# First scores from rows summed in place, and the softmax shift as a bias in every exponential

## The chip, the cores and the metric

The kernel runs on one NeuronCore of a Trainium2 chip. The core has five engines that run beside each other and meet through semaphores: TensorE (matmul; "PE" in a profile, its weight loads "PEld"), VectorE ("DVE"), ScalarE ("ACT"), GpSimd ("POOL") and SyncE ("SP"). Transfers are issued from the queues of SP, ACT and POOL. The metric is the device time of one execution in microseconds: 1229.62 us, the median of three runs (1228.37 to 1229.89).

## The reference

Two independent parts are computed, and their results are put side by side in the last axis. Everything is float32.

```python
# part A: a state-space convolution, L = 2048, D = 576, N = 128
dt = exp(log_dt)[:, None]; logdA = dt * (A_re + 1j*A_im); dB = dt * (B_re + 1j*B_im)
K = einsum("dn,dnl,dn->dl", C, exp(logdA[:, :, None] * l), dB).real
y = irfft(rfft(pad(u)) * rfft(pad(K)))[:L] + u * Dskip
# part B: attention with 32 query heads of 18 columns and one shared head of keys and values, S = 2048
q = (x @ wq).reshape(B, S, 32, 18); k = x @ wk; v = x @ wv
p = softmax(einsum(q, k) * 18 ** -0.5)
out = (p @ v).reshape(B, S, 576) @ wo
```

## The kernel before

**Attention.** The 2048 queries are worked in four chunks `c` of 512, the heads in 16 pairs, the keys in 16 blocks `kb` of 128. One step of the inner loop is a head pair and a key block: two score matmuls write a PSUM tile `s` of 128 keys by 2 x 512 queries (`scores`, L446), one ScalarE instruction takes exp of all 1024 columns into `P` (`exponentials`, L455 and L457), and four matmuls by 256 columns, twice, multiply `P` by the values into `ops` (`product`, L755). There are 1024 such steps. Three score tiles exist (`NS = 3`), so steps are issued in rounds of three: the scores of a round, then products of earlier rounds and filler work, then the next round. A score matmul has to wait until the exponential that read its tile three steps ago has ended. Eight `P` tiles exist (`NP`).

Scores are computed with operands split in a rounded part and a rest: the rows of `kaug` hold kh, kl, kh (18 rows each, keys) and the rows of `aug` hold qh, qh, ql (queries), twice, at partitions 0 and 64, one for each head of a pair. Row 54 of `kaug` is one and row 54 of `aug` is minus an upper bound of the scores, so that the shift of the softmax comes out of the matmul itself: 55 rows. Only the first two head pairs of the first chunk take the shift as `bias=self.nb` (L455). The bound comes from the largest key and query magnitudes (`kmax`, `ab`), through a small matmul `up`, its maximum `un`, and a running maximum `u` over all units so far.

**Convolution.** It is cut into 12 blocks of 48 channels. `front` makes the kernel K from factors (`factors`: an exponential of dt, products by VectorE, two sines and an exponential on ScalarE), tables (`tables`) and matmuls (`kgen`); `back` transforms u and K with matmuls by `dft`, multiplies on VectorE, and transforms back.

**What sets the order.** The order on TensorE, ScalarE and VectorE is the one in which the program issues (`manual_schedule`). In the loop, `main` keeps a model clock (`Clock`) with a price for every operation (an exponential costs 0.925 in it), and a planner fills the time that this clock leaves on TensorE with query projections, output projections and convolution work, in pieces (`Stream`). The constants at the top (`RATE`, `CAP`, `LEAST` and others) steer it. Set-up is written out by hand: `Attention.setup` issues the transfers, keeps TensorE busy with three `cold` matmul sets, projects keys (`kps`), values (`vps`) and the first 126 query columns (`qps`) over five pieces `k` of the model axis, then places keys and queries into `kaug` and `aug` by transfers (L306, L393). `conv.begin` interleaves the first ten pieces of the first convolution block. `values` transposes the values, and then `main` begins.

A `matmul4` is one product of 128 columns as four matmuls of 32 columns, which run side by side; `project` does the same with the four chunks of x.

Of the kernel before, what the change touches and what calls it, by code (L numbers as in the profile page):

```python
# [32 lines left out]
NS = 3  # L33
NP = 8


RATE = 1.7223
PACE = 2.6661
AHEAD = 0.6441
TOTAL = 238.4006  # L40
LAST = 660.2161
DEFER = 0.3799
NAUG = 5
LEFT = 1.0372
CAP = 0.5454
DEBT = 0.8847
GROUP = 0.2874
HOLD = 0.3303
LEAD = 0.8335
MOST = 0.7745  # L50
LEAST = 0.5036
NEAR = 0.4134
SLOPE = 0.2673
SOON = 0.5397
URGENT = 7.3595
GAP = 0.2175
GAP_NEW = 0.6686
# [50 lines left out]
class Vector:  # L108
# [21 lines left out]
    def reciprocal(self, out, src):  # L130
        self.k.dve(out, 6.5e-3)
        return self.v.reciprocal(out, src)

# [55 lines left out]
class Attention:  # L189
# [36 lines left out]
    def setup(self, tp, conv):  # L226

# [3 lines left out]
        self.sel = cp.tile([P, 8], F32, name="sel_sb")  # L235
        spread = tp.tile([P, 130], F32, name="spread_sb")
# [3 lines left out]
        self.kmax = cp.tile([P, 1], F32, name="kmax")  # L240
        wkv = tp.tile([P, 6, 64], F32, name="wkv_sb")
        xr = tp.tile([P, 4, 3, CT], F32, name="xr")
# [8 lines left out]
        self.nb = cp.tile([P, 1], F32, name="nb")  # L251
        self.x0 = x0 = self.xp.tile([P, 5, CT], F32, name="x0", tag="x")

        V.memset(cold, 0.0)
        conv.early()
        nc.sync.dma_start(wkv, a["wkv"])
        for k in range(4):
            nc.sync.dma_start(x0[:, k, :], a["xT"][0, :, k, :])
            nc.sync.dma_start(xr[:, k], a["xT"][1:4, :, k, :].rearrange("c p n -> p c n"))
            if k == 0:  # L260
                nc.scalar.dma_start(self.wq[0], a["wq"][0, :, :, :MT[0][1]])
        nc.sync.dma_start(x0[:, 4, :], a["xe"][0])
        nc.sync.dma_start(xe, a["xe"][1])
        nc.scalar.dma_start(self.sel, a["sel"][:, 0:8])
        nc.scalar.dma_start(spread, a["sel"][:, 8:138])
        for t in self.ring[:2]:
            for b in (32, 96):
                nc.gpsimd.memset(t[b:b + 32, :].bitcast(F32), 0.0)
        for b in (54, 118):
            nc.gpsimd.dma_start(self.kaug[b:b + 1, :], a["ones"])  # L270
# [3 lines left out]
        self.ubound, self.first = None, True  # L274
        self.aug = {n: self.ring[n % NAUG] for n in range(64)}
        self.ready, self.od, self.qd = set(), {}, {}
# [4 lines left out]
        conv.begin()  # L281
        fps = self.bank(CT, "cold")
        for _ in range(3):
            matmul4(nc, fps, cold[:, 0:P], cold)
        kps, self.qps = (self.ps_s.tile([P, 2, CT], F32, tag="s", name=n)[:, 0, :] for n in ("kps", "q0_0"))
        self.pv = pv = self.ps_o.tile([P, CT], F32, tag="o", name="vps")

        def project(ps, j, k):
            for c in range(NCH):
                w = wkv[:, 4 + c // 2 if k == 4 else k, j:j + 32]  # L290
                x = (xe if c % 2 else x0[:, 4, :]) if k == 4 else xr[:, k, c - 1, :] if c else x0[:, k, :]
                nc.tensor.matmul(ps[32 * c:32 * c + 32, :], w, x, start=(k == 0), stop=(k == 4), tile_position=(0, 32 * c))
        for k in range(5):
            project(kps, 0, k)
            matmul4(nc, self.qps, self.wq[0][:, k, :], x0[:, k, :], start=(k == 0), stop=(k == 4))
            if k < 2:
                project(pv, 32, k)
        nc.scalar.activation(kh, kps, AF.Copy)
        V.tensor_reduce(km[:, 4:5], kps, axis=AX.X, op=ALU.max, apply_absolute_value=True)
        V.tensor_scalar(km[:, 0:4], spread[:, 126:130], km[:, 4:5], None, op0=ALU.mult)  # L300
        V.tensor_tensor(kl, kps, kh.bitcast(F32), op=ALU.subtract)

        def place(c):
            for r, t in ((0, kh), (36, kh), (18, kl)):
                for b in (0, 64):
                    nc.sync.dma_start(self.kaug[b + r:b + r + 18, c * CT:(c + 1) * CT].bitcast(F32), t[32 * c:32 * c + 18, :].bitcast(F32))  # L306
        place(0)
        pk = self.bank(4, "kmx")
        nc.tensor.matmul(pk[:126, :], spread[:, 0:126], km[:, 0:4], start=True, stop=True)
        for k in range(2, 4):  # L310
            project(pv, 32, k)
        self.side_work = side = Stream(self.side(), self.k, 99.0)
        while self.first:
            side.advance()
        V.tensor_reduce(self.kmax[:126, :], pk[:126, :], axis=AX.X, op=ALU.max)
        while 1 not in self.ready:
            side.advance()
        for c in range(1, NCH):
            place(c)
        side.advance()  # L320

# [3 lines left out]
        project(pv, 32, 4)  # L325
        V.tensor_copy(self.vt, pv)
# [44 lines left out]
    def first_queries(self, ps):  # L371
        nc, V, mn = self.nc, self.V, MT[0][1]
        qh, ql, ab = self.keys[:, 3, :], self.keys[:, 4, :], self.p2.tile([P, 3], F32, tag="ab", name="ab0_0")
        nc.scalar.activation(qh[:mn, :], ps[:mn, :], AF.Copy)
        V.tensor_tensor(ql[:mn, :], ps[:mn, :], qh[:mn, :].bitcast(F32), op=ALU.subtract)
        V.tensor_reduce(ab[:mn, 0:1], ps[:mn, :], axis=AX.X, op=ALU.max, apply_absolute_value=True)
        yield from self.queries(0, 0, qh, ql, ab[:, 0:1])

    def queries(self, c, m, qh, ql, ab):
# [4 lines left out]
        if m == 0:  # L384
            self.qd[c] = self.dr.tile([H, 55, CT], F32, tag="qd", name=f"qd{c}")
        qd = self.qd[c]

        n0 = 4 if (c, m) == (0, 0) else 0
        for row, src in ((0, qh), (18, qh), (36, ql)) if n0 else ():
            for h in range(n0):  # L390
                b = 64 * (h % 2) + row
                q = nc.gpsimd if h // 2 == 1 else nc.scalar if row < 36 else nc.sync
                q.dma_start(self.aug[h // 2][b:b + 18, :].bitcast(F32), src[h * DH:h * DH + DH, :].bitcast(F32))  # L393
# [5 lines left out]
        self.first = False  # L399
        yield "v", 0.0, False  # L400
        aw = self.p2.tile([P, P], F32, tag="aw", name=f"aw{c}_{m}", bufs=1)
        V.tensor_scalar(aw[:mn, :], ab[:mn, 0:1].broadcast_to([mn, P]), self.kmax[:mn, 0:1], None, op0=ALU.mult)
# [3 lines left out]
        matmul4(nc, up, aw[:mn, :], self.sel[:mn, 0:8])  # L406
# [5 lines left out]
        if self.ubound is not None:  # L412
            u2 = self.p2.tile([P, 1], F32, tag="u2", name=f"u2_{c}_{m}", bufs=4)
            V.tensor_tensor(u2, un, self.ubound, op=ALU.max)
            un = u2
        self.ubound = un
        if n0:
            V.tensor_scalar(self.nb, un, -SCALE, None, op0=ALU.mult)
        sh = self.p2.tile([8, CT], F32R, tag="sh", name=f"sh{c}_{m}", bufs=1)
        V.tensor_scalar(sh, un[0:8, 0:1].broadcast_to([8, CT]), -1.0, None, op0=ALU.mult)  # L420
        self.ready.update(range(n0 // 2))
        q = nc.gpsimd if n0 == 0 else nc.sync
        if n0:
            yield "w", 0.0, False
            store(q)
        q.dma_start(qd[h0 + n0:h1, 54, :], sh[:h1 - h0 - n0, :].bitcast(F32))
        self.queried = c * H + h1

    def fetch(self, group):

        while self.next < min(64, 2 * group + NAUG) and 2 * self.next + 2 <= self.queried:
            c, pr = divmod(self.next, 16)
            t = self.aug[self.next]
            for j in range(2):
                self.nc.sync.dma_start(t[64 * j:64 * j + 55, :].bitcast(F32), self.qd[c][2 * pr + j])
# [3 lines left out]
    def scores(self, i, c, pr, kb, cost):  # L439
# [4 lines left out]
        for j in range(2):  # L444
            r = slice(64 * j, 64 * j + 55)
# [4 lines left out]
    def exponentials(self, i, c, pr, kb, ps, ready, free):  # L450
# [3 lines left out]
        if 16 * c + pr < 2:  # L454
            nc.scalar.activation(pt, ps, AF.Exp, scale=SCALE, bias=self.nb)  # L455
        else:
            nc.scalar.activation(pt, ps, AF.Exp, scale=SCALE)  # L457
# [158 lines left out]
    def side(self):  # L616
# [3 lines left out]
        yield from self.first_queries(self.qps)  # L620
# [67 lines left out]
    def main(self, conv, flag):  # L688
# [3 lines left out]
        self.load_wo()  # L692
        K.t = K.v = K.a = self.o_free = 0.0
# [76 lines left out]
        for r in range(0, len(pairs), NS):  # L770
            new = range(r, min(r + NS, len(pairs)))
            self.step = new[-1] // 2
            ss = {}
            for i in new:
# [4 lines left out]
                ss[i] = self.scores(i, c, 2 * g + j, kb, 0.335 if i == r else 0.215)  # L779
# [43 lines left out]
        nc.vector.tensor_scalar(flag, self.ubound[0:1, :], LIMIT / (2 * SCALE), None, op0=ALU.is_le)  # L823
# [86 lines left out]
class Conv:  # L910
# [21 lines left out]
    def setup(self):  # L932
# [3 lines left out]
        self.pos = cp.tile([P, 2, NF], F32, name="pos_sb")  # L936
# [7 lines left out]
    def load(self, k, q=None):  # L944
# [5 lines left out]
        raw = self.p0.tile([P, 6, ND], F32, tag="raw", name=f"raw{k}")  # L950
        dt = self.p0.tile([P, ND], F32, tag="dt", name=f"dt{k}")
        q.dma_start(dt, self.a["ldt"][k * ND:(k + 1) * ND].partition_broadcast(P))
        q.dma_start(raw, self.a["prm"][k])
        self.raw[k] = raw, dt

    def load_u(self, k):
# [3 lines left out]
        ut = self.p0.tile([P, 4, NE], F32, tag="u", name=f"u{k}")  # L960
        if k < 2:
            nc.vector.memset(ut[0:1, 0, 0:1], 0.0)
        dsk = self.p0.tile([P, NE], F32, tag="dsk", name=f"dsk{k}")
        nc.sync.dma_start(ut, self.a["u"][k])
        nc.sync.dma_start(dsk, self.a["dsk"][k].partition_broadcast(P))
        self.ut[k] = ut, dsk
        self.ut_ready[k % 2] = self.k.t + 10.0

    def factors(self, k):
# [4 lines left out]
        raw, dt = self.raw.pop(k)  # L974
# [38 lines left out]
        if k == 0:  # L1013
            nc.scalar.activation(m, m, AF.Exp)
# [130 lines left out]
    def back(self, k, kt):  # L1145
        nc, V, p1, K = self.nc, self.V, self.p1, self.k
        tt = V.tensor_tensor
        ut, dsk = self.ut.pop(k)
# [73 lines left out]
    def early(self):  # L1222
        nc = self.nc
        nc.scalar.dma_start(self.pos, self.a["pos"])
# [4 lines left out]
    def begin(self):  # L1229

        for _ in range(10):
            self.streams[0].advance()
# [141 lines left out]
```

## Time and profile before

| | |
|---|---|
| median of three runs | 1229.62 us |
| profiled execution | 1230.26 us, of which span 1228.0 us |
| mean granted TensorE clock | 0.982 |
| TensorE busy | 1154.1 us (94%) |
| ScalarE busy | 1053.9 us (86%) |
| VectorE busy | 994.9 us (81%) |
| first exponential of the loop starts | 32.81 us |
| last one ends | 1200.88 us |

A row of a group view reads: line, engine, operation, output tile <- input tiles, shapes, count | busy us, mean ns of one | idle time of the engine before them and what ended it. A row of the order of time begins with start and duration in us. An engine name with a q is its queue, which issues transfers. The span is cut into slices or stretches where work by stage is wanted; the granted clock is 1.00 at full speed. Busy time of TensorE overlaps between neighbours, so it is an upper estimate of its work.

### The profile page before, as it was taken

The numbers are of one execution on the slowest core, as the hardware profiler recorded it, in microseconds if no ns is written. First come the engines' busy times: TensorE is split into PE (matmuls) and PEld (weight loads), VectorE is DVE, ScalarE is ACT, GpSimd is POOL, SyncE is SP. The second block draws the span as 40 slices with busy tenths as digits, with TensorE's granted clock in tenths as the row PEclk, the third lists the DMA queues.
The fourth block names the chain that finished last, engine by engine and source line by source line (L and its number), as shares of the span: only waits on it lengthen the run. The fifth ranks groups of instructions, "written<-read, shape, count | busy, mean of one in ns | idle before, by whom it ended". The sixth has DMA issues, their size and how long they took to land.

```text
span 1228.0 us, 40862 instructions
## 1 busy us (share of the span) xinstructions
PE 1154.1 (94%) x17882; PEld 609.0 (50%) x17882; DVE 994.9 (81%) x1674; ACT 1053.9 (86%) x1101; POOL 53.7 (4%) x93
## 2 busy tenths in 40 slices
PE   7999899899899899999899999999989899999997
PEld 1455455455445455455454545555545445455544
DVE  4757996996997897896798698898799799698493
ACT  2789899989888989989887989999988989999991
POOL 2000100100100000000010000000010000000000
PEclk8899999999999999999999989999999999999999
DMA  7532312123242112113033300212222211112201
GB/s 231 160 105 65 108 53 84 36 63 91 67 125 78 51 48 82 36 50 108 25 93 105 95 15 34 83 35 77 78 68 87 78 41 53 63 34 77 63 28 55
DMA packets 55082, 89.84 MB, mean 73 GB/s; under 512 B 14172, under 2 KB 24796, under 8 KB 54387
## 3 DMA queue, kind: packets, MB, share of 16 engines
q1 hardware_dynamic: 43911, 72.46, 18.2%
q0 software_dynamic: 10016, 13.98, 4.4%
q8 instruction: 142, 2.33, 0.8%
q10 hardware_dynamic: 972, 0.74, 0.2%
q14 instruction: 41, 0.34, 0.1%
HBM read 49.28 MB, written 36.50 MB: 70 GB/s over the span
## 4 chain that ended last, share of the span: by engine, by line
PE 66%; DVE 23%; DMA 4%; issue 3%; ACT 3%; SPq 0%; DVEq 0%; ACTq 0%
PE ops L755 25%; PE s L446 18%; PE op L186 5%; PE q L186 4%; DVE ks L116 3%; PE iy L186 3%; PE kg L1082 3%; DVE tab L116 3%; DVE acc L116 2%; ACT P L457 2%; DVE f L116 1%; PE lk L186 1%; PE hu L186 1%; PE hk L186 1%; PE fin L186 1%
## 5 line engine op out<-in xcount | busy, mean ns | idle before, releaser
L457 ACT ACTIVATE P<-s 128x1024 f32<-128x1024 f32 x992 | 942.4, 1028 | 118.1 <-PE s L446 111.4
L755 PE MATMUL ops<-P,v_sb 128*32 128x256 f32 x8192 | 533.2, 382 | 7.9 <-DVE o L120 7.7
L446 PE MATMUL s<-aug,kaug 55*128 55x512 f32 x2048 | 350.9, 439 | 10.8 <-ACT P L457 5.7
L755 PEld LDWEIGHTS ops<-P,v_sb 128*32 128x32 f32 x8192 | 255.9, 110 | 181.0 <-issue 35.0
L446 PEld LDWEIGHTS s<-aug,kaug 55*128 55x128 f32 x2048 | 168.0, 185 | 205.3 <-ACT P L457 100.7
L186 PE MATMUL q<-x,wq_sb 128*32 128x256 f32 (+2 forms) x1480 | 116.2, 413 | 21.8 <-DVE ql L116 14.6
L186 PEld LDWEIGHTS q<-x,wq_sb 128*32 128x32 f32 (+2 forms) x1480 | 48.8, 113 | 71.0 <-issue 40.0
L186 PE MATMUL op<-wo_sb,oT 126*32 126x288 f32 (+1 forms) x1024 | 76.7, 415 | 5.1 <-DVE scu L116 2.5
L116 DVE TENSOR_TENSOR tab<-tab,tt 128x576 f32<-128x576 f32 (+1 forms) x72 | 59.2, 822 | 1.9
L120 DVE COPY ksb<-kg 128x192 f32<-128x192 f32 x48 | 17.5, 364 | 53.1 <-PE kg L1082 52.9
L116 DVE TENSOR_TENSOR tab<-tab 128x576 f32<-128x576 f32 (+1 forms) x72 | 59.0, 819 | 1.2
L116 DVE TENSOR_TENSOR tt<-f,sum 128x576 f32<-128x576 f32 (+1 forms) x72 | 58.7, 816 | 0.0
L116 DVE TENSOR_TENSOR tab<-sum,r 128x576 f32<-128x576 f32 (+1 forms) x72 | 58.7, 815 | 0.0
L116 DVE TENSOR_TENSOR tab<-r,dif 128x576 f32<-128x576 f32 (+1 forms) x72 | 58.7, 815 | 0.0
L396 POOL DMA_DIRECT2D qd<-qh x38 | 24.0, 636 | 733.4 <-DVE qh L120 733.4
L116 DVE TENSOR_TENSOR acc<-acc,pt 128x1728 f32<-128x1728 f32 (+2 forms) x36 | 48.6, 1349 | 0.3
L116 DVE TENSOR_TENSOR pt<-us,ks 128x1728 f32<-128x1728 f32 (+2 forms) x36 | 48.6, 1350 | 0.2
L186 PEld LDWEIGHTS op<-wo_sb,oT 126*32 126x32 f32 (+1 forms) x1024 | 28.9, 110 | 38.7 <-issue 16.9
L116 DVE TENSOR_TENSOR sck<-lk,sck 128x384 f32<-128x384 f32 x48 | 24.5, 551 | 27.8 <-PE lk L186 27.8
L455 ACT ACTIVATE P<-s,nb 128x1024 f32<-128x1024 f32 x32 | 33.1, 1116 | 13.5 <-PE s L446 13.4
L1082 PEld LDWEIGHTS kg<-tab 128*32 128x32 f32 x2304 | 35.8, 110 | 16.5 <-issue 7.4
L1082 PE MATMUL kg<-tab 128*32 128x64 f32 x2304 | 42.1, 220 | 2.0 <-DVE tab L116 0.8
(132 smaller groups left out, 1004.9 us busy)
## 6 DMA issues: line engine op xcount, KB each, us to landing
aug<-qd SPq DMA_DIRECT2D x124, 110.0 KB
od<-o SPq DMA_DIRECT2D x31, 256.0 KB
qd<-qh POOLq DMA_DIRECT2D x30, 252.0 KB, 5.7
u<-u SPq DMA_DIRECT2D x12, 384.0 KB
kd<-ksb SPq DMA_DIRECT2D x12, 384.0 KB
kt<-kd SPq DMA_DIRECT2D x48, 96.0 KB
outa<-u SPq DMA_DIRECT2D x12, 384.0 KB
oT<-od SPq DMA_DIRECT2D x16, 252.0 KB
```

What stands on the lines that cost most here:

```text
L116: return self.v.tensor_tensor(out, *a, **k)
L120: return self.v.tensor_copy(out, *a, **k)
L186: nc.tensor.matmul(ps[j:e], w[:, j:e], x, start=start, stop=stop, tile_position=(0, j))
L396: q.dma_start(qd[h0 + n0:h1, row:row + 18, :], src[n0 * DH:mn, :].bitcast(F32))
L446: nc.tensor.matmul(ps[:, j, :], self.kaug[r, kb * P:(kb + 1) * P], t[r, :], start=True, stop=True)
L455: nc.scalar.activation(pt, ps, AF.Exp, scale=SCALE, bias=self.nb)
L457: nc.scalar.activation(pt, ps, AF.Exp, scale=SCALE)
L755: nc.tensor.matmul(o_ps[32 * j:32 * j + 32, cs], self.v[:, kb, :], pts[2 * n + j // 2][:, j % 2, cs], start=(kb + f == 0), stop=(kb + f == ...
L1082: nc.tensor.matmul(ps[32 * g:32 * g + 32, d, :], t[:, :32], t[:, 32:], start=(j == 0), stop=(j == 1), tile_position=(0, 32 * g))
```

## The change

- **Direct rows.** In set-up, three weight tiles `direct` of 128 columns are made: `direct[0]` holds wk three times for each half (with minus wk in the second place), `direct[1]` and `direct[2]` hold wq of heads 0, 1 and 2, 3 in the same way (minus in the third place). GpSimd zeroes them, VectorE copies the columns. Three more `matmul4` for each k sum x times these into `first` tiles, which have the layout of `kaug` and `aug` already. ScalarE copies each sum in rounded form, and one VectorE instruction with a column of 0 and -1 turns the marked rows into the rest. The transfers that placed chunk 0 of the keys and the first four heads go; those for key chunks 1 to 3 stay, half on SP and half on POOL.
- **Order in set-up.** wkv first, then all of chunk 0 of x, then the other chunks (`xr`). TensorE does four cold sets instead of three, then for each k three direct sums and `qps`, and after that keys and values. The scores of the first two steps (`early`) are issued behind the keys. On VectorE the copies for `direct[1]` and `direct[2]` stand behind `conv.begin(7)`.
- **Shift as bias.** Row 54 goes from `kaug`, `aug` and the stored queries (54 rows). Every exponential takes `bias=self.nb[:, m]`, a column for each unit of 126 query columns, made by one instruction with a running minimum; `sh` and `u2` go, and the tile `aw` shrinks from 128 to 8 columns.
- **Fewer early transfers.** `sel` joins `pos` in one tensor, `ldt` joins `prm`, `dsk` joins `u`, `ones` goes, and `wo` is loaded at the loop's step 60 instead of at its start.
- **Constants of the planner.** Twenty of them get other values, and its clocks start at 2.5 and 0.4 for VectorE and ScalarE.

```diff
-RATE = 1.7223
-PACE = 2.6661
+COLD = 4
+RATE = 1.9482
+PACE = 2.0109
...
-LEFT = 1.0372
-CAP = 0.5454
+LEFT = 1.2228
+CAP = 0.9396
...
-        V.memset(cold, 0.0)
+        nc.sync.dma_start(wkv, a["wkv"])
         conv.early()
-        nc.sync.dma_start(wkv, a["wkv"])
         for k in range(4):
             nc.sync.dma_start(x0[:, k, :], a["xT"][0, :, k, :])
-            nc.sync.dma_start(xr[:, k], a["xT"][1:4, :, k, :].rearrange("c p n -> p c n"))
...
+        def rows(t, src, minus):
+            t = t.rearrange("p k (j c) -> p k j c", j=2)
+            for r in range(3):
+                if r == minus:
+                    V.tensor_scalar(t[:, :, :, 18 * r:18 * r + 18], src, -1.0, None, op0=ALU.mult)
+                else:
+                    V.tensor_copy(t[:, :, :, 18 * r:18 * r + 18], src)
+        rows(direct[0], wkv[:, 0:5, 0:DH].unsqueeze(2).broadcast_to([P, 5, 2, DH]), 1)
+        conv.begin(7)
+        for j in range(2):
+            rows(direct[1 + j], self.wq[0][:, :, 36 * j:36 * j + 36].rearrange("p k (j d) -> p k j d", j=2), 2)
+        conv.begin(3)
...
         for k in range(5):
+            for ps, w in zip(sums, direct):
+                matmul4(nc, ps, w[:, k, :], x0[:, k, :], start=(k == 0), stop=(k == 4))
+            matmul4(nc, qps, self.wq[0][:, k, :], x0[:, k, :], start=(k == 0), stop=(k == 4))
+        for j, (ps, t) in enumerate(zip(sums, (self.kaug[:, 0:CT], self.ring[0], self.ring[1]))):
+            nc.scalar.activation(t, ps, AF.Copy)
+            V.scalar_tensor_tensor(t, ps, spread[:, 130 + (j > 0):131 + (j > 0)], t.bitcast(F32), op0=ALU.mult, op1=ALU.add)
+        V.tensor_reduce(ab[:mn, 0:1], qps[:mn, :], axis=AX.X, op=ALU.max, apply_absolute_value=True)
+        conv.begin(1)
+        for k in order[:3]:
             project(kps, 0, k)
+            project(pv, 32, k)
+        project(kps, 0, 4)
+        project(kps, 0, 3)
+        self.early = {i: self.scores(i, 0, i, 0, 0.0) for i in range(2)}
...
+        for c in range(1, NCH):
             for r, t in ((0, kh), (36, kh), (18, kl)):
                 for b in (0, 64):
+                    (nc.sync if b else nc.gpsimd).dma_start(...)
...
-        sh = self.p2.tile([8, CT], F32R, tag="sh", name=f"sh{c}_{m}", bufs=1)
-        V.tensor_scalar(sh, un[0:8, 0:1].broadcast_to([8, CT]), -1.0, None, op0=ALU.mult)
+        i = 5 * c + m
+        V.tensor_scalar(self.nb[:, i:i + 1], un, -SCALE, self.nb[:, i - 1:i] if i else None, op0=ALU.mult, **(dict(op1=ALU.min) if i else {}))
...
-        if 16 * c + pr < 2:
-            nc.scalar.activation(pt, ps, AF.Exp, scale=SCALE, bias=self.nb)
-        else:
-            nc.scalar.activation(pt, ps, AF.Exp, scale=SCALE)
+        m = 5 * c + min((2 * pr + 1) // 7, 4)
+        nc.scalar.activation(pt, ps, AF.Exp, scale=SCALE, bias=self.nb[:, m:m + 1])
...
+            if r == 40 * NS:
+                self.load_wo()
```

More of the change, by code (lines that the diff above doesn't have):

```diff
@@ L280, in setup @@
         self.todo, self.busy, self.group = [], False, 0
-        conv.begin()
+        def rows(t, src, minus):
[10 more added lines that the diff above has]
+        conv.begin(3)
         fps = self.bank(CT, "cold")
-        for _ in range(3):
+        for _ in range(COLD):
             matmul4(nc, fps, cold[:, 0:P], cold)
-        kps, self.qps = (self.ps_s.tile([P, 2, CT], F32, tag="s", name=n)[:, 0, :] for n in ("kps", "q0_0"))
-        self.pv = pv = self.ps_o.tile([P, CT], F32, tag="o", name="vps")
+        first = [self.ps_s.tile([P, 2, CT], F32, tag="s", name=f"first{j}") for j in range(3)]
+        sums = [first[0][:, 0, :], first[0][:, 1, :], first[1][:, 0, :]]
+        kps, qps = first[2][:, 0, :], first[2][:, 1, :]
+        pv = self.ps_o.tile([P, CT], F32, tag="o", name="vps")
+        order = (0, 1, 2, 4, 3)
         def project(ps, j, k):
@@ L300, in setup @@
         V.tensor_scalar(km[:, 0:4], spread[:, 126:130], km[:, 4:5], None, op0=ALU.mult)
+        pk = self.bank(4, "kmx")
+        nc.tensor.matmul(pk[:126, :], spread[:, 0:126], km[:, 0:4], start=True, stop=True)
+        project(pv, 32, 4)
+        project(pv, 32, 3)
+        nc.scalar.activation(qh[:mn, :], qps[:mn, :], AF.Copy)
+        V.tensor_reduce(self.kmax[:126, :], pk[:126, :], axis=AX.X, op=ALU.max)
+        self.kb = self.p2.tile([P, P], F32, tag="aw", name="kmaxb", bufs=1)
+        V.tensor_copy(self.kb[:126, :], self.kmax[:126, 0:1].broadcast_to([126, P]))
+        self.side_work = side = Stream(self.side(qh, ql, ab), self.k, 99.0)
+        while self.queried == 0:
+            side.advance()
         V.tensor_tensor(kl, kps, kh.bitcast(F32), op=ALU.subtract)
-        def place(c):
+        V.tensor_tensor(ql[:mn, :], qps[:mn, :], qh[:mn, :].bitcast(F32), op=ALU.subtract)
+        V.tensor_copy(self.vt, pv)
+        for c in range(1, NCH):
             for r, t in ((0, kh), (36, kh), (18, kl)):
                 for b in (0, 64):
[L306 to L319, printed above, removed]
+                    (nc.sync if b else nc.gpsimd).dma_start(self.kaug[b + r:b + r + 18, c * CT:(c + 1) * CT].bitcast(F32), t[32 * c:32 * c + 18, :].bitcast(F32))
         side.advance()
@@ L384, in queries @@
         if m == 0:
-            self.qd[c] = self.dr.tile([H, 55, CT], F32, tag="qd", name=f"qd{c}")
+            self.qd[c] = self.dr.tile([H, 54, CT], F32, tag="qd", name=f"qd{c}")
         qd = self.qd[c]
         n0 = 4 if (c, m) == (0, 0) else 0
[L389 to L393, printed above, removed]
         def store(q):
@@ L614, in finish, with side @@
                 add(t, nh)
-    def side(self):
+    def side(self, *first):
         xts = {0: self.x0}
         units = [(c, m) for c in range(NCH) for m in range(5)]
-        yield from self.first_queries(self.qps)
+        yield from self.queries(0, 0, *first)
         for c, m in units[1:]:
@@ L935, in setup @@
         self.dft = cp.tile([P, 2048], F32, name="dft_sb")
-        self.pos = cp.tile([P, 2, NF], F32, name="pos_sb")
+        self.con = cp.tile([P, 2 * NF + 8], F32, name="con_sb")
+        self.pos = self.con[:, 0:2 * NF].rearrange("p (j n) -> p j n", j=2)
         self.hp = cp.tile([P, 1], F32, name="hp_sb")
@@ L1227, in early, with begin @@
         self.streams = [Stream(self.front(0), self.k)]
-    def begin(self):
-        for _ in range(10):
+    def begin(self, n):
+        for _ in range(n):
             self.streams[0].advance()
```

151 lines of the change are left out of this document (67 added, 84 removed).

## The prediction

> **What bounds the kernel now.** I read the page's busy shares and chain first, then the groups by line, then ScalarE's and TensorE's order of time in set-up and in an ordinary stretch, then the work by stretch. The page, busy shares, granted clock by slice, and chain by engine:
>
> ```profile
> PE 1154.1 (94%) x17882; PEld 609.0 (50%) x17882; DVE 994.9 (81%) x1674; ACT 1053.9 (86%) x1101; POOL 53.7 (4%) x93
> PEclk8899999999999999999999989999999999999999
> PE 66%; DVE 23%; DMA 4%; issue 3%; ACT 3%; SPq 0%; DVEq 0%; ACTq 0%
> ```
>
> TensorE is the bound, ScalarE stands 14% of the span idle, and set-up is the one place where the clock is low for long. The groups that the change touches, and who ScalarE waits for:
>
> ```profile
> L457 ACT ACTIVATE P<-s 128x1024 f32<-128x1024 f32 x992 | 942.4, 1028 | 118.1 <-PE s L446 111.4 <-PE ops L755 0.6
> L455 ACT ACTIVATE P<-s,nb 128x1024 f32<-128x1024 f32 x32 | 33.1, 1116 | 13.5 <-PE s L446 13.4
> L1011 ACT ACTIVATE r<-r,hp_sb 128x1248 f32<-128x1248 f32 x12 | 16.0, 1336 | 8.2 <-DVE r L124 8.1
> L1012 ACT ACTIVATE f<-f 128x1248 f32<-128x1248 f32 x12 | 14.7, 1228 | 0.0
> L124 DVE TENSOR_SCALAR sh<-u 8x512 fp32r<-8x512 f32 x19 | 7.9, 416 | 1.0 <-DMA qd<-sh 0.4
> L116 DVE TENSOR_TENSOR u<-un,u 128x1 f32<-128x1 f32 x18 | 2.9, 159 | 0.6
> L124 DVE TENSOR_SCALAR aw<-ab,kmax 126x128 f32<-126x128 f32 (+1 forms) x20 | 5.8, 289 | 0.7
> L120 DVE COPY tab<-r 128x192 f32<-128x192 f32 x48 | 10.0, 249 | 0.0
> ```
>
> The reader should see two things. The exponential with a bias tile (`nb`) takes 1116 ns, the one without 1028; the two sines, of one shape, differ the same way. And ScalarE's 118 us of idle time before exponentials is nearly all waiting for scores.
>
> Set-up in order of time (start, duration, engine, line, tiles):
>
> ```profile
> 1.51 5.07 PE L186 MATMUL cold<-cold 128*32 128x512 f32 x24 [1.51 <-DVE cold L135]
> 4.25 1.28 ACT L975 ACT_TABLE_LOAD   x1 [4.25 <-DMA pos_sb<-pos]
> 6.56 0.24 ACT L975 ACTIVATE dt<-dt 128x48 f32<-128x48 f32 x1 [1.02 <-DMA dt<-ldt]
> 8.69 0.36 DVE L116 TENSOR_TENSOR raw<-raw,dt 128x192 f32<-128x192 f32 x1 [7.00 <-DMA raw<-prm]
> 15.34 0.81 DVE L124 TENSOR_SCALAR r<-f 128x1248 int32<-128x1248 int32 x1
> 10.60 1.07 PE L292 MATMUL kps<-xr,wkv_sb 128*32 128x512 f32 x3 [3.17 <-DMA xr<-xT]
> 23.80 0.69 DVE L128 TENSOR_REDUCE km<-kps 128x1 f32<-128x512 f32 x1 [7.65 <-ACT keys L298]
> 31.42 2.25 PE L446 MATMUL s<-aug,kaug 55*128 55x512 f32 x6 [3.24 <-DMA kaug<-keys]
> 32.81 3.12 ACT L455 ACTIVATE P<-s,nb 128x1024 f32<-128x1024 f32 x3 [8.18 <-PE s L446]
> 33.60 1.11 PE L332 MATMUL vp<-ident,keys 128*128 128x128 f32 x4
> ```
>
> and the same stage as work by stretch (busy us of each engine, granted clock, DMA share, GB/s):
>
> ```profile
> 10.00:16.00 6.00, 5.40 (x28) 1.39 (x32) 5.87 (x6) 0.00 (x0) 0.00 (x0) 0.50 1.05 388
> 16.00:24.00 8.00, 7.97 (x70) 1.91 (x62) 0.35 (x2) 5.59 (x5) 0.00 (x0) 0.97 0.74 249
> 31.00:40.00 9.00, 8.03 (x48) 4.15 (x48) 5.15 (x7) 3.46 (x4) 0.00 (x0) 0.50 0.21 52
> 40.00:46.00 6.00, 5.71 (x78) 2.73 (x76) 5.93 (x14) 5.81 (x6) 0.00 (x0) 0.97 0.19 46
> ```
>
> TensorE loses set-up time in three ways: it waits for x until 10.60, it runs at clock 0.50 from 10 to 16 and from 31 to 40, and it waits 3.24 us for the rows of kaug.
>
> **The change, part by part. 1: set-up.** One group here is a `matmul4` or one `project` with 512 columns: four matmuls side by side in two passes, eight records. The chain in order of time shows what four records cost, first at clock 0.50, then at full clock:
>
> ```profile
> 12.53 0.85 PE q L186 x4
> 19.68 0.43 PE q L186 x4
> ```
>
> So a group takes 0.86 us at full clock and 1.70 at half. Before, set-up has 15 groups (five each of kps, q, vps). The change keeps them and adds three `matmul4` for each of five k: 15 groups, 12.9 us at full clock. The fourth cold set adds 1.7 us (5.07 / 3), covered by the wait that follows. What leaves is the DMA hop from keys to kaug and aug for the first chunk (3.24 us on TensorE).
>
> When can TensorE begin? Sum 0 needs wkv only. Sums 1 and 2 need `direct[1]` and `direct[2]`, which VectorE, in written order, makes after `conv.begin(7)`. That work runs in the trace from 8.69 to 16.15: 7.46 us. In front of it stands the exponential of dt, now in the `raw` transfer, second on ACT's queue. In the trace the second transfer there (dt) let its exponential start at 6.56 and raw let VectorE start at 8.69. I take 6.56 + 0.24, so VectorE at 6.85; bounds are the first landing that ScalarE's rows show (4.25) plus the exponential, 2.4 us earlier, and 8.69 plus 0.24, 2.1 us later. Then 6.85 + 7.46 + three copies of 180 elements (by the 249 ns row, 0.75) = 15.0 us for sum 1. TensorE ends its cold sets at 1.5 + 6.8 = 8.3, does one group, and stands for over 5 us. It stood 3.17 us before 10.60 and the clock was 0.50 to about 16.4 (0.97 over the stretch from 16); so I let it restart slow again and lose half of 5.8 us, 2.9.
>
> From 15.0: 19 groups at 0.86 = 16.3, plus 2.9, gives 34.2. Three k of kps and vps and the last two of kps are 8 groups, 6.9: keys' sum at 41.1, before 23.2. Then VectorE: 0.69 + 0.24, the small matmul, kmax, its copy and aw (0.15 to 0.3 each), to about 43.1; `up` behind the last two vps groups at 44.4; un and nb to 44.8, where the first exponential starts (before 32.81). The copy to `vt` comes only after kl and ql, three times 0.69: 46.8; TensorE idles 2.1 us there. The transposes take 0.55 at full clock (1.11 in the trace at 0.50): done at 47.4. Before, the same state is reached at 33.60 + 1.11 = 34.7, but half of the 5.6 us up to about 40.3 (0.97 over the stretch from 40) is lost to the clock, so 37.5 in comparable time. Difference: **+9.9 us**. At its best (VectorE 2.4 us earlier, no slow clock) it is 9.9 − 2.4 − 2.9 = +4.6, at its worst +12.
>
> The Trainium skill weighs in on the clock: "TensorE: Matmul & The Clock Gate", Part 1, says a busy window of about 3.4 us gives full clock back. The trace shows 5.8 us of slow work after 10.60, so the measurement decides; by the rule the loss would be 1.7 instead of 2.9 and the time 1.2 us less.
>
> The chunks 1 to 3 of kaug now go half on SP, half on POOL, nine issues each; SP's queue before took 13.32 us for 18:
>
> ```profile
> 30.32 13.32 SPq L306 DMA_DIRECT2D kaug<-keys  x18
> 53.21 4.95 SPq L338 DMA_DIRECT2D wo_sb<-wo  x5
> 69.53 0.85 PE L446 MATMUL s<-aug,kaug 55*128 55x512 f32 x2 [0.30 <-DMA aug<-qd]
> ```
>
> Nine take about 6.7, behind kl at 45.4, so the last land near 52; chunk 1 is wanted by the ninth exponential, some 9 us after 44.8, so exponentials hide it; without that cover a chunk costs 2.2. Behind these issues SP holds the query store, wq and dft, all far from due. wo leaves the queue in front of the first aug fetch: −0.3 (the wait shown); at step 60 its five issues (4.95 us) can hold up a fetch there, which is issued a group ahead: 0.
>
> **2: a bias on all exponentials.** 992 more take `nb`. Runs without a break give the price in the pipeline, and work by stretch shows what surrounds it:
>
> ```profile
> 39.67 6.14 ACT L455 ACTIVATE P<-s,nb 128x1024 f32<-128x1024 f32 x6 [3.74 <-PE s L446]
> 73.22 2.86 ACT L457 ACTIVATE P<-s 128x1024 f32<-128x1024 f32 x3 [1.07 <-PE s L446]
> 79.76 2.86 ACT L457 ACTIVATE P<-s 128x1024 f32<-128x1024 f32 x3 [0.52 <-PE s L446]
> 101.39 2.85 ACT L457 ACTIVATE P<-s 128x1024 f32<-128x1024 f32 x3 [0.19 <-PE s L446]
> 1199.86 1.02 ACT L457 ACTIVATE P<-s 128x1024 f32<-128x1024 f32 x1 [0.64 <-PE s L446]
> 46.24:69.12 22.88, 22.42 (x380) 11.64 (x376) 15.73 (x33) 21.68 (x21) 2.45 (x4) 1.00 0.82 248
> ```
>
> With bias (6.14 − 1.116) / 5 = 1.005 us from start to start; without (2.86 − 1.028) / 2 = 0.916. So 0.089 us each: 992 × 0.089 = 88 us more ScalarE work, 0.27 us a round of three. The idle time before a round is 0.19 to 0.52 us: it hides 0.27 in a long round, not in a short one. Bounds: 0 (all hidden in the 118 us) and 88 (none). The nearest row is the stretch where the bias already stands and TensorE has work in plenty, 46.24 to 69.12: 22.88 / 21 = 1.090 us for each exponential. The whole loop ran from 32.81 to 1200.88, 1168.1 us. ScalarE's other work in it is 11 sets of two sines, two table loads and two small exponentials; beside the rows above:
>
> ```profile
> 1062.86 1.26 ACT L1008 ACTIVATE m<-m 128x1248 f32<-128x1248 f32 x1
> 1064.13 1.28 ACT L1011 ACT_TABLE_LOAD   x1
> ```
>
> 1.34 + 1.23 + 2 × 1.28 + 1.26 + 0.24 = 6.6 us a set, 73 us in all; 1095 / 1024 leaves 1.069. The difference of 0.021 on 992 is **+20.4 us**, and I take it: ScalarE is 95% busy in that stretch, and the loop would have to hold that throughout.
>
> **3: what leaves VectorE.** sh and u (19 × 0.416 + 18 × 0.159 = 10.8 us) and most of aw (19 × 0.15 = 2.9): 13.7 us. VectorE is 23% of the chain, so 13.7 × 0.23 = **−3.2**; ends 0 and −13.7.
>
> **4: at nothing.** 54 rows for 55 in scores: columns set a matmul's time, and 512 stay. u and its skip factor in one transfer, and 19 fewer small stores on POOL's queue: both hidden by engines that wait for neither. The planner's constants: they order filler work, not its amount. The longest sum of waits of TensorE on VectorE is that of the query groups,
>
> ```profile
> PE q L186 <- DVE ql L116: 14.6, 6, 3.0
> ```
>
> so a better or worse order is worth up to 14.6 us either way; I take 0 and keep it for the range.
>
> Sum, against the profiled execution (1230.26, of which 1228.0 is span; the runs' median is 0.6 lower): 1230.3 + 9.9 − 0.3 + 20.4 − 3.2 = **1257 us**.
>
> **Rivals.** A: the bias hides wholly, for 118 us of idle exceed 88. For it: rounds with 0.52 us before them. Against: rounds with 0.19. Set-up remains: 1230.3 + 9.9 − 0.3 − 3.2 = 1237 us. B: the order written for 0.925 us an exponential (the planner's price) leaves every round short. A round's third score needs the third exponential's buffer, and that score holds the products behind it; half of 0.27 on 331 rounds is 45 us: 1230.3 + 9.6 + 45 − 3.2 = 1282. C, faster: VectorE is the hidden bound. Its 13.7 us sit in chains that hold the shared PSUM bank, all of it counts, and the bias hides: 1230.3 + 4.6 (the best set-up) − 0.3 − 13.7 = 1221. It decides once more than about two thirds of the 13.7 reaches the loop's end with set-up at its best; the 14.6 us of waits speak for it, the 23% against. D: direct rows do start the first exponentials earlier, as said. For that, TensorE would need its first 20 groups done by 32.8 − 3.7 − 6.9 = 22; they take 17.2 us and cannot begin before the cold sets end at 8.3. I count it out as a case and inside C's set-up.
>
> **How the numbers follow.** Forecast 0.5 (its own range 1245 to 1270, from set-up +4.6 to +12 and half to one and a half times the 20.4), A 0.18, B 0.14, C 0.18. The range goes to B's far side and to A's near one: 1231 to 1286, leaving out C and a little of B. About 0.2% is what a measurement tells from no change. Faster 0.17 (C, less a tenth), same 0.03 (between A and C), slower 0.8.
>
> **What the profile after would show.** Right: first exponential near 45 us; TensorE idle before the sums until about 15 and slow after it; 1116 ns at all 1024 exponentials; ScalarE over 92% busy in the loop, its wait for scores down to half of 111 us, and more waits of scores for exponentials than now. Wrong, if the sums start by 10 us; if exponentials with bias take 1028; or if the loop from first to last exponential stays within 1168 us, which is A, or drops below 1155, which is C.

## The result, and the profile after

The changed kernel takes 1258.5 us (median of four runs, 1257.0 to 1262.6) against 1229.8 before: 1.0235 times as long, 95% interval 1.0203 to 1.0268. The forecast was 1257. The profiled execution took 1257.44 us, its span 1255.7. The page after, with busy shares, clock and chain, then the one group of exponentials and the scores' row:

```profile
PE 1180.2 (94%) x18010; PEld 612.3 (49%) x18010; DVE 993.4 (79%) x1668; ACT 1137.1 (91%) x1104; POOL 42.1 (3%) x74
PEclk9999999999999999999999999999999999999999
PE 66%; DVE 19%; ACT 8%; issue 4%; DMA 2%; SPq 0%; ACTq 0%; POOL 0%; DVEq 0%
L454 ACT ACTIVATE P<-s,nb 128x1024 f32<-128x1024 f32 x1024 | 1057.9, 1118 | 59.0 <-PE s L445 48.8
L445 PE MATMUL s<-aug,kaug 54*128 54x512 f32 x2048 | 376.7, 450 | 20.9 <-ACT P L454 17.1
```

The scores' row of the kernel before:

```profile
L446 PE MATMUL s<-aug,kaug 55*128 55x512 f32 x2048 | 350.9, 439 | 10.8 <-ACT P L457 5.7
```

ScalarE's busy time grew by 83 us (1053.9 to 1137.1). It now stands in the chain with 8% where it had 3%. Its waits for scores before all 1024 exponentials fell from 125 us (111.4 and 13.4 in the two groups before) to 49, and scores wait for exponentials 17.1 us where they waited 5.7. ScalarE stands less and holds TensorE more: the two are coupled more tightly.

Set-up in order of time, after:

```profile
5.19 0.24 ACT L972 ACTIVATE raw<-raw 128x48 f32<-128x48 f32 x1 [1.26 <-DMA raw<-prm]
12.11 0.81 DVE L125 TENSOR_SCALAR r<-f 128x1248 int32<-128x1248 int32 x1
13.56 3.40 PE L191 MATMUL first<-x,direct 128*32 128x512 f32 x16 [5.26 <-DVE direct L121]
34.01 0.62 PE L306 MATMUL first<-x,wkv_sb 128*32 128x512 f32 x1 [2.46 <-DVE ab L129]
41.78 0.69 DVE L129 TENSOR_REDUCE km<-first 128x1 f32<-128x512 f32 x1 [7.83 <-ACT keys L324]
45.70 3.12 ACT L454 ACTIVATE P<-s,nb 128x1024 f32<-128x1024 f32 x3 [2.60 <-DMA kaug<-keys]
47.43 0.63 PE L355 MATMUL vp<-ident,keys 128*128 128x128 f32 x4
```

TensorE stands 5.26 us for the rows that VectorE makes, as the forecast had it. The keys' sum is there at 41.1, the first exponential starts at 45.70 (44.8 forecast, 32.81 before). One wait was not forecast: 2.46 us before the keys, because the keys' sum takes the other half of the score tile from which VectorE still reads the first queries for `ab`.

The loop as one stretch, from the first exponential's start to the last one's end, of the kernel before and then of the changed one:

```profile
32.81:1200.88 1168.07, 1109.79 (x17418) 592.20 (x17419) 973.30 (x1624) 1044.10 (x1090) 46.44 (x76) 0.99 0.23 69
```

```profile
45.70:1228.26 1182.56, 1124.72 (x17399) 588.46 (x17403) 968.90 (x1615) 1125.67 (x1090) 36.40 (x60) 1.00 0.22 68
```

So the span grew by 27.7 us (1228.0 to 1255.7): 12.9 of later start, 14.5 of longer loop, and 0.3 in the tail behind the loop (27.1 to 27.4). ScalarE is busy 89.4% of the loop before (1044.10 / 1168.07) and 95.2% after.

### The profile page after: what moved, and what is told of

The parts are those of the page before. It is cut to its first block, busy times and chain, and to the rows that moved or that the text cites. A ratio compares the mean times of both kernels' runs of the same rounds, so it can differ in the third digit from the quotient of the medians.

```text
span 1255.7 us, 40985 instructions
## 1 busy us (share of the span) xinstructions
PE 1180.2 (94%) x18010; PEld 612.3 (49%) x18010; DVE 993.4 (79%) x1668; ACT 1137.1 (91%) x1104; POOL 42.1 (3%) x74
## 4 chain that ended last, share of the span: by engine, by line
PE 66%; DVE 19%; ACT 8%; issue 4%; DMA 2%; SPq 0%; ACTq 0%; POOL 0%; DVEq 0%
PE ops L752 24%; PE s L445 20%; ACT P L454 8%; PE op L191 5%; PE q L191 3%; DVE ks L117 3%; PE iy L191 3%; PE kg L1080 3%; DVE acc L117 2%; DVE tab L117 2%; DVE f L117 2%; PE lk L191 1%; PE first L191 1%; PE lu L191 1%; PE hu L191 1%
## 5 line engine op out<-in xcount | busy, mean ns | idle before, releaser
L454 ACT ACTIVATE P<-s,nb 128x1024 f32<-128x1024 f32 x1024 | 1057.9, 1118 | 59.0 <-PE s L445 48.8
L445 PE MATMUL s<-aug,kaug 54*128 54x512 f32 x2048 | 376.7, 450 | 20.9 <-ACT P L454 17.1
L445 PEld LDWEIGHTS s<-aug,kaug 54*128 54x128 f32 x2048 | 166.5, 184 | 256.5 <-ACT P L454 186.0
L191 PE MATMUL q<-x,wq_sb 128*32 128x256 f32 (+2 forms) x1440 | 101.0, 390 | 20.4 <-DVE ql L117 14.4
L191 PEld LDWEIGHTS q<-x,wq_sb 128*32 128x32 f32 (+2 forms) x1440 | 44.3, 109 | 61.8 <-issue 36.3
L117 DVE TENSOR_TENSOR pt<-us,ks 128x1728 f32<-128x1728 f32 (+2 forms) x36 | 48.6, 1350 | 0.2
L191 PEld LDWEIGHTS op<-wo_sb,oT 126*32 126x32 f32 (+1 forms) x1032 | 28.8, 109 | 33.9 <-issue 17.1
L117 DVE TENSOR_TENSOR ks<-ks 128x576 f32<-128x576 f32 (+1 forms) x48 | 41.1, 856 | 1.0
```

What stands on the lines that cost most here:

```text
L117: return self.v.tensor_tensor(out, *a, **k)
L191: nc.tensor.matmul(ps[j:e], w[:, j:e], x, start=start, stop=stop, tile_position=(0, j))
L445: nc.tensor.matmul(ps[:, j, :], self.kaug[r, kb * P:(kb + 1) * P], t[r, :], start=True, stop=True)
```

## The experiments

Four theories were to be told apart: the forecast (set-up costs by its added matmuls, the bias by the coupling of two nearly full engines); that the bias hides and the planner's new order is what lengthens the loop; that nothing of the bias hides in a round; and that VectorE is the hidden bound.

The changed kernel was timed once, beside a kernel before of 1229.8 us; the kernel before was timed again with each series of runs, at medians of 1229.1, 1228.3, 1228.0 and 1227.6. A difference from the changed kernel's 1258.5 is therefore good to about 2 us. Where it matters, the same difference by the ratios, each to the kernel before of its own series, stands beside it.

**The bias, taken off and put on.** Off in the changed kernel:

```diff
-        nc.scalar.activation(pt, ps, AF.Exp, scale=SCALE, bias=self.nb[:, m:m + 1])
+        if 16 * c + pr < 2:
+            nc.scalar.activation(pt, ps, AF.Exp, scale=SCALE, bias=self.nb[:, m:m + 1])
+        else:
+            nc.scalar.activation(pt, ps, AF.Exp, scale=SCALE)
```

> The changed kernel with the bias taken off the exponentials of all head pairs but the first two (the softmax is then taken without a shift there, which leaves its ratio as it was); order of all engines unchanged. My theory: 992 exponentials lose 0.089 us, the loop gives back some 20 us: 1236 to 1242, what is left over the kernel before is set-up. Rival A (the bias hides in ScalarE's idle time and the loop is longer by the planner's new order): 1254 to 1260. Rival B (nothing of the bias hides in a round): below 1220.

Measured: 1236.2 us (seven runs, 1231.1 to 1239.6), 22.3 less than the changed kernel (24.4 by the ratios), as the theory had it; in the profiled executions the loop from first to last exponential is 1161.8 against 1182.6, 20.8 less:

```profile
48.53:1210.29 1161.76, 1107.77 (x17396) 592.87 (x17400) 967.17 (x1615) 1044.03 (x1090) 36.33 (x60) 0.99 0.22 69
```

On in the kernel before, as a tile of zeros:

```diff
+        self.zero = cp.tile([P, 1], F32, name="zero")
+        nc.gpsimd.memset(self.zero, 0.0)
...
-            nc.scalar.activation(pt, ps, AF.Exp, scale=SCALE)
+            nc.scalar.activation(pt, ps, AF.Exp, scale=SCALE, bias=self.zero)
```

> The kernel before with a bias tile of zeros on the 992 exponentials that had none; nothing else. My theory: +15 to +25, so 1245 to 1255. Rival A: within 3 us of 1230. Rival B: +45, so 1275.

Measured: 1254.3 us, ratio 1.0204 (1.0165 to 1.0243), 25 more than before, again as the theory had it. The groups of exponentials, with the bias off, and with it on:

```profile
L457 ACT ACTIVATE P<-s 128x1024 f32<-128x1024 f32 x992 | 942.3, 1028 | 113.0 <-PE s L445 103.4
```

```profile
L459 ACT ACTIVATE P<-s,zero 128x1024 f32<-128x1024 f32 x992 | 1024.9, 1118 | 62.5 <-PE s L448 54.4
```

Values of zero cost the same 1118 ns, so it is the operand that costs, 90 ns. 82.6 us of added ScalarE work (1024.9 − 942.3) became 25 us of time: idle time hid two thirds. The start of the n-th exponential in this run, less its start in the kernel before, shows that it is paid all along the loop:

```
exponential    0    96   240   384   528   672   816   960  1023
us later    -1.3   1.4   5.3   7.4  11.8  14.3  18.1  21.6  24.3
```

From the first to the last that is 25.6 us, 0.026 for each of the 992, where the forecast took 0.021 from a 23 us stretch of early rounds.

Something works the other way in the changed kernel. Its profiled loop holds three stretches of 3.4 us at half clock, that of the run with the bias off nine; over all executions the mean granted clock is 0.991 to 0.993 with the bias and 0.983 to 0.991 without it. So the 22.3 us seem to be what is left of the bias's price after a better clock; that is argued, not shown. What brings that clock on stays open: zeros in the kernel before did not (0.985 to 0.987, against 0.983 to 0.990 beside it).

**The planner's constants, exchanged.** The twenty constants of the kernel before in the changed kernel, and those of the changed one in the kernel before:

```diff
-RATE = 1.9482
+RATE = 1.7223
...
-GAP_NEW = 0.5805
+GAP_NEW = 0.6686
```

> The changed kernel with the twenty planner constants of the kernel before. My theory has the constants at 0: 1255 to 1262. Rival: the new constants fit the order to the new loop and hide part of the bias: 1264 to 1280. Second rival: they are part of the loss: 1245 to 1253.

> The kernel before with the twenty planner constants of the changed one. My theory: 1227 to 1234. Rival (constants are what lengthens the loop by some 15 us): 1242 to 1248. The opposite rival (they are better by themselves): 1218 to 1225.

Measured: 1272.7 us (1271.9 to 1274.7) for the first, 14.2 above the changed kernel; 1243.3 (1240.0 to 1248.3) for the second, 1.0124 times the kernel before (1.0078 to 1.0170). In both runs the first rival came true and the theory missed. But neither set is dear as such: each fits its own kernel and costs the other 14 us. With the old ones on the changed kernel, most of it lies behind the last exponential (tail 40.8 us against 27.4); with the new ones on the kernel before, 5.8 us lie there (32.9 against 27.1) and 6.3 in the loop. Who ScalarE waits for, with the old constants, and after:

```profile
ACT o_last L584 <- DVE rc_last L583: 19.6, 2, 18.0
```

```profile
ACT o_last L584 <- DVE rc_last L583: 6.4, 2, 4.8
```

`o_last` stands behind the last convolution block on VectorE, and that block was still at work after the loop's end.

**Set-up: VectorE's order, and the added matmuls.** Rows first:

```diff
         rows(direct[0], wkv[:, 0:5, 0:DH].unsqueeze(2).broadcast_to([P, 5, 2, DH]), 1)
-        conv.begin(7)
         for j in range(2):
             rows(direct[1 + j], ...)
+        conv.begin(7)
         conv.begin(3)
```

> The changed kernel with VectorE making direct[1] and direct[2] before the seven pieces of the first convolution block instead of after them. My theory (TensorE stands 5.3 us behind VectorE at 8.3 to 13.56 us, then runs 3.4 us at half clock): first exponential 6 to 7 us earlier, time 1251 to 1254. Rival (only the added matmuls and the bias cost; ScalarE sets the pace later, so an earlier start is lost again): 1257 to 1260.

Measured: 1253.1 us (1252.0 to 1256.0), 5.4 less (3.9 by the ratios). Sums and first exponential in order of time:

```profile
7.62 2.95 PE L191 MATMUL first<-x,direct 128*32 128x512 f32 x24
10.22 1.22 PE L191 MATMUL first<-x,wq_sb 128*32 128x512 f32 x8
40.87 3.12 ACT L454 ACTIVATE P<-s,nb 128x1024 f32<-128x1024 f32 x3 [2.60 <-DMA kaug<-keys]
```

The sums begin at 7.62 without a break and at full clock. The first exponential comes 4.8 us earlier and not 6 to 7: behind the sums TensorE was busy 1.17 of 3.40 us, and the clock fell to half from 27.4 to 30.8. At the last exponential 2.8 us of the lead are left.

One piece of the sums instead of five:

```diff
             for ps, w in zip(sums, direct):
-                matmul4(nc, ps, w[:, k, :], x0[:, k, :], start=(k == 0), stop=(k == 4))
+                if k == 0:
+                    matmul4(nc, ps, w[:, k, :], x0[:, k, :])
```

> The changed kernel with the direct sums taken over the first of the five pieces of the model axis alone (four fifths of these sums are left out, so the first keys and the first four heads are not the reference's): 12 groups of matmuls at 0.86 us less. My theory: 10.3 us less, 1246 to 1251. Rival (the sums hide behind transfers or VectorE): 1256 to 1260.

Measured: 1246.5 us (1246.4 to 1247.9), 12.0 less (10.5 by the ratios); first exponential 11.8 us earlier, and 11.1 of it is left at the last one:

```profile
33.92 3.12 ACT L455 ACTIVATE P<-s,nb 128x1024 f32<-128x1024 f32 x3 [2.60 <-DMA kaug<-keys]
```

The added matmuls are paid in full, and in set-up nothing covers them.

**VectorE's work put back.**

```diff
+        nc.vector.tensor_tensor(u2, un, un, op=ALU.max)
...
+        nc.vector.tensor_scalar(sh, un[0:8, 0:1].broadcast_to([8, CT]), -1.0, None, op0=ALU.mult)
```

> The changed kernel with two VectorE instructions of the sizes of u and sh put back behind nb in each of the 20 units, read by nobody, priced at nothing in the planner so that the order stays: 11.5 us more VectorE work. My theory (a quarter of it is on the path): +1 to +5, 1259 to 1263. Rival C (all of it counts): 1268 to 1272. Nothing: 1257 to 1259.

Measured: 1266.4 us (1263.9 to 1270.8), 7.9 more (9.8 by the ratios), between the two theories; by the times alone, that all 11.2 us count is not excluded. In the profiled execution 2.9 of its 7.4 us at the last exponential were there at the first one (the clock was at half for 10.2 instead of 3.4 us of set-up), and the loop is 4.6 us longer (1187.15 against 1182.56). The two groups are 11.2 us:

```profile
L427 DVE TENSOR_SCALAR sh<-un 8x512 fp32r<-8x512 f32 x20 | 8.2, 408 | 0.0
L425 DVE TENSOR_TENSOR u<-un 128x1 f32<-128x1 f32 x20 | 3.0, 150 | 0.0
```

**The slow clock of the kernel before, filled.** Four cold sets behind set-up:

```diff
         project(pv, 32, 4)
         V.tensor_copy(self.vt, pv)
+        fps = self.bank(CT, "warm")
+        for _ in range(4):
+            matmul4(nc, fps, cold[:, 0:P], cold)
```

> The kernel before with four more cold sets at the end of set-up, where TensorE waits for kaug and the clock falls to half from 30 to 40 us. My theory of the slow clock (half of 8.9 us is lost there, less 0.3 us by which the sets may end late): 1224 to 1227. Rival (the loop is not bound by TensorE there): 1229 to 1231.

Measured: 1233.4 us (twelve runs, 1226.6 to 1242.1), ratio 1.0037 (1.0015 to 1.0060): slower, both theories missed. The same places in order of time, then clock and work from 30 to 40 and from 50 to 60:

```profile
33.33 0.66 PE L335 MATMUL vp<-ident,keys 128*128 128x128 f32 x4
55.98 1.08 PE L186 MATMUL q<-x,wq_sb 128*32 128x256 f32 x8 [4.17 <-DMA wq_sb<-wq]
30.00:40.00 10.00, 9.07 (x96) 4.06 (x88) 5.84 (x9) 6.19 (x7) 0.00 (x0) 1.00 0.20 52
50.00:60.00 10.00, 5.72 (x50) 2.45 (x52) 7.37 (x10) 4.54 (x6) 0.54 (x1) 0.71 1.00 340
```

The clock was full from 30 to 40, and TensorE came to the third piece of wq before it had landed; there it stood 4.17 us and the clock fell again. So the next run also brings forward what stands in front of wq in SP's queue:

```diff
-                    nc.sync.dma_start(self.kaug[...
+                    (nc.gpsimd if c and b == 0 else nc.sync).dma_start(self.kaug[...
...
-        self.load_wo()
...
+            if r == 40 * NS:
+                self.load_wo()
```

> The kernel before with the four cold sets in the wait for kaug, and two more things that the change brings: half of the places of key chunks 1 to 3 on POOL's queue, and wo loaded at step 60. Theory (the cold sets did win the slow clock back, 4 us, and the third wq piece, 9 us behind in SP's queue, took it away again): without that wait 1222 to 1226. Rival (an earlier start is lost to whatever is late next): 1228 to 1234.

> The same without the cold sets: the kernel before with half of the places on POOL's queue and wo at step 60. Theory (both hidden before, but for the 0.3 us wait): 1226 to 1230. Rival (the transfers were worth something by themselves): 1220 to 1224.

Measured: 1227.9 us with the cold sets (ratio 1.0003, 0.9984 to 1.0023) and 1226.6 without (0.9988, 0.9974 to 1.0002). The first missed its theory and came out level with the kernel before, at the edge of its rival's range; the second came out as its theory had it. The first one's early gain is in the trace, and is gone later:

```
exponential                        0    48   288   528   768   864   912  1023
cold sets and queues, us later  -0.8  -4.5  -6.4  -7.0  -4.0  -0.8   0.9   0.9
queues alone, us later          -0.2  -2.0  -2.6  -1.6  -1.8  -1.8  -1.8  -1.8
```

The late steps are about 1.7 us each. One of them, as work by stretch of the run with cold sets:

```profile
971.50:974.90 3.40, 1.66 (x28) 0.57 (x24) 1.55 (x4) 3.37 (x4) 0.00 (x0) 1.00 0.02 5
974.90:978.30 3.40, 3.23 (x24) 1.69 (x27) 2.85 (x6) 3.37 (x4) 0.00 (x0) 0.50 0.00 0
```

After 3.4 us in which TensorE was busy less than half (ScalarE had sines), it ran the next 3.4 us at half clock. Where these stretches fall differs between executions; the loop with the cold sets has nine stretches of 3.4 us at half clock, that of the queues alone seven. Two more are 3.4 of the 5.2 us that the cold sets lose against the queues alone between the 48th and the last exponential. Whether the earlier start brought them on, or chance did, stays open.

**Both losses off.** No bias and VectorE's rows first, the first edits of two runs above together:

> The changed kernel without bias on the 992 exponentials and with VectorE's rows first: both losses taken away. If they add: 1236 less 5.4, so 1229 to 1233, no better than the kernel before, and what is left is the added matmuls less what the change's queues and constants win. If they don't add: 1234 to 1238.

Measured: 1227.4 us (1224.4 to 1230.3), ratio 0.9991 (0.9977 to 1.0004): level with the kernel before and below both ranges. It is 3.4 us below what the two savings add up to (1258.5 − 22.3 − 5.4 = 1230.8); by the ratios only 1.7, near the edge of the interval. So the two savings add, as far as these times can tell.

**A version that beats both.** The kernel before with only the queues changed, and the shift dropped where it stood in row 54; the stores of `sh`, the row of ones and four of GpSimd's zero fills go with it; the planner keeps the price of `sh`, so the order stays:

```diff
-        sh = self.p2.tile([8, CT], F32R, tag="sh", name=f"sh{c}_{m}", bufs=1)
-        V.tensor_scalar(sh, un[0:8, 0:1].broadcast_to([8, CT]), -1.0, None, op0=ALU.mult)
+        K.v += 0.085 + 0.5e-3 * CT
+        K.work += 0.085 + 0.5e-3 * CT
...
-        q.dma_start(qd[h0 + n0:h1, 54, :], sh[:h1 - h0 - n0, :].bitcast(F32))
```

> The kernel of the run with only the queues changed, and besides the shift dropped where it stood in row 54 (54 rows, no sh and no stores of it, no row of ones; softmax ratios stay, the bound is still tested at the end and the first two head pairs keep their bias). The planner still counts the price of sh, so the order of all engines stays. If VectorE's 7.9 us of sh are worth what the 11.5 us of the run with VectorE's work put back showed: 1227 less 3 to 5, so 1221 to 1224, better than both kernels. If they hide: 1225 to 1228.

Measured: 1222.8 us (1218.2 to 1223.7), ratio 0.9950 (0.9933 to 0.9966). Against the run with queues alone the lead grows from 0.6 us at the first exponential to 5.0 at the last. How much of that is VectorE's `sh` and how much the stores and fills that left with it was not tested apart. The bound is tested at the end in any case (`flag`), and below it an exponential without a shift stays within 30 in its argument.

## Why the prediction was right

- **Set-up, +9.9: right in its mechanism.** VectorE's chain, the stand of TensorE before the sums and the order behind them are in the trace at the places given. Sum 1 came at 13.56 instead of 15.0, since dt landed at about 5.2 and not 6.56, and the slow clock after it lasted to 16.4, about 3 us instead of 5.8. That was worth 3 us less; the wait of 2.46 for `ab`, which the sum lacked, took most of it back. That the keys' sum came at 41.1 to the tenth is luck: these two misses cancel. The transposes end at 48.06, forecast 47.4. The slow clock differs between executions: in three others with the same set-up (bias off, old constants, VectorE's work put back) it took 10.2 us of set-up instead of 3.4, and the first exponential started at 48.1 to 48.6. The two sizes were shown apart: 12 of the 15 groups are worth 12.0 us (10.5 by the ratios, 10.3 by the count), VectorE's order 5.4 (3.9 by the ratios), with the first exponential 4.8 earlier (6 to 7 expected).
- **The credit of 2.8 us for the kernel before's slow clock from 30 to 40: not shown.** Taking the slow clock away won 2.5 us at the 48th exponential (with queues against queues alone) and nothing at the end.
- **The bias, +20.4: right, a little low.** 22.3 taken off, 25 put on; the better clock beside it was not foreseen. The price of 0.089 was 0.090. The early stretch gave 1.090 us an exponential; the loop after, without the 73 us of sines, shows (1182.56 − 73) / 1024 = 1.084. Rival A (all hidden) falls by both runs, rival B (45 us) too.
- **VectorE's relief, −3.2: both factors off, and the product near by luck.** The forecast took a quarter of 13.7 us. But the 13.7 count `u` as gone, while an instruction for `nb` takes its place in 19 units, and `aw` became shorter by 1.2 us and not 2.9. In the groups of the profile after:

```profile
L125 DVE TENSOR_SCALAR nb<-un,nb 128x1 f32<-128x1 f32 x19 | 4.1, 214 | 0.7
L125 DVE TENSOR_SCALAR aw<-con_sb,ab 126x8 f32<-126x8 f32 (+1 forms) x20 | 4.6, 230 | 0.6
```

So some 8 us left (7.9 of `sh`, 2.9 of `u`, 1.2 of `aw`, less 4.1). The share that counts is larger than the chain's 23%: 11.2 us put back cost 4.6 in the loop and 7.9 in the medians, a share of 0.4 to 0.7, and 7.9 us of `sh` taken out of the kernel before, with its stores, gave 3.8. An estimate from these shares is 3.2 to 5.6 us of relief. The changed kernel's loop without the bias, 6.3 us shorter than before (1161.8 against 1168.1), agrees, though it holds the new constants too. Rival C falls as a whole: it needed the bias hidden and the best set-up.
- **The constants at 0: the step whose reason failed.** Exchanged alone they are worth 14 us: the changed kernel loses as much with the old ones as the kernel before with the new. The forecast held that they "order filler work, not its amount"; but the order decides what is left for the tail. Zero fitted all the same, since each kernel was timed with constants that fit it (tails of 27.1 and 27.4 us); the forecast did not argue from that, so it is luck. With the old ones the changed kernel's 1272.7 would have been 16 above the sum.
- **At nothing: mostly so.** Queues and the later wo, put into the kernel before, gave 1.4 us with an interval that reaches no change.

## What to carry to other kernels

An operand that adds a tenth to every instruction of the second busiest engine is not hidden because that engine idles as much in total (here a third of the added time came through): look at the rounds, and take the rate from a stretch where the dearer form already runs. The matmuls added to this set-up cost their full time, for there was no other work yet to cover them, and a wait on another engine's written order came on top. Before an instruction is counted as gone, look for the one that takes its place. Where an order is written from fitted constants, a change of the work is to be judged with constants fitted to it; exchanging them between the two kernels shows how much of a difference they are.

## What was not expected of the hardware

The clock fell to half for 3.4 us, or two or three times that, after stretches of 3.4 us in which TensorE was busy less than half, and not only after full idleness: 1.66 of 3.40 us above. In set-up of the kernel before the same is seen before its long slow stretch:

```profile
26.70:30.10 3.40, 1.49 (x20) 0.22 (x16) 1.73 (x12) 0.00 (x0) 1.45 (x3) 1.00 0.46 134
30.10:33.50 3.40, 2.08 (x6) 1.25 (x6) 0.00 (x0) 0.69 (x1) 0.00 (x0) 0.50 0.21 57
33.50:37.00 3.50, 2.95 (x25) 1.52 (x28) 2.25 (x3) 2.43 (x3) 0.00 (x0) 0.50 0.19 48
37.00:40.30 3.30, 3.30 (x26) 1.38 (x18) 3.20 (x6) 0.63 (x1) 0.00 (x0) 0.50 0.22 55
```

One half is no limit, though. In the changed kernel TensorE was busy 1.45 of 3.40 us from 30.1 to 33.5 and the clock stayed full; with one piece of the sums it fell behind the stretch from 417.1 to 420.5, where TensorE was busy 2.33 of 3.40. What else than the busy time of the profile decides it stays open.

The Trainium skill's "TensorE: Matmul & The Clock Gate", Part 1, gives a free-running window of 3.4 us and a full clock after one busy window. The changed kernel's set-up agrees: 3.4 us slow from 13.0 to 16.4, TensorE busy 2.84 of them. So the loss there was 1.4 us, nearer to the 1.7 that the prediction set aside than to its 2.9. In the kernel before the slow stretches are two and three windows long (9.6 to 16.4, 30.1 to 40.3). TensorE was busy 2.40, 2.08 and 2.95 us in the windows behind which the clock stayed at half, and without a break in those behind which it rose. That fits the rule only if a window busy in part can fail to count, and 2.84 and 2.95 us on either side show no share from which one counts.
